# First dense products ahead of the second scores in the steps with few value groups; three value groups and the start of pair 7 moved into the first two steps

## The chip, the cores and the metric

The kernel runs on one core of a Trainium2 chip. Five engines work side by side, each through its own list of instructions in order: PE (matrix products; its weight loads are listed apart as PEld), DVE and ACT (elementwise work, reductions, copies out of PSUM), POOL (elementwise work in SBUF) and SP, which only issues DMAs. Time is device microseconds (us) of this core; the result of a kernel is the median of several runs. The profile is of one further execution.

## The reference, cut to what matters

```python
def _A_ref(x, mem0, Wq, Wk, Wv, Wo, seg_len):      # S=2048, Dm=512, H=32 heads of 128, M=8, seg 32
    mem = mem0
    for s in range(n_seg):                          # 64 segments
        h = concat([mem, x[:, 32*s:32*s+32]])       # 8 memory rows + 32 tokens
        q, k, v = h @ Wq, h @ Wk, h @ Wv
        p = softmax(mask(q k^T * scale))
        o = (p @ v) @ Wo
        mem = o[:, :8];  outs.append(o[:, 8:])
    return concat(outs)
def _B_ref(x, w1, w2):
    return relu(x @ w1) @ w2                        # 512 -> 1376 -> 512
x = x + _A_ref(layernorm(x), ...);  x = x + _B_ref(layernorm(x), ...)
x = x + _A_ref(layernorm(x), ...);  x = x + _B_ref(layernorm(x), ...)
```

The memory rows make the attention a recurrence over 64 segments, and there are two such layers with the same weights. Arithmetic is bf16 with f32 sums.

## The kernel before, in words

**Steps.** Step k (`step`, k = 1 to 67, after `first_step` for k = 0) does segment k of the first attention layer ("layer 0") and segment k-4 of the second ("layer 1") together, each 8 memory rows and 32 tokens. Steps 1 to 3 have layer 0 alone and steps 64 to 67 layer 1 alone (`single`). Beside the attention a step does the dense layer of the rows finished two steps before (`dense_h(k - 2)`, `dense_y(k - 2)`). What links one step to the next is `output_mem` (L564, tile wo: the memory rows' output product), a copy on ACT (L750, tile wm), a small turn on PE (L756, tile mt) and copies into HT and HTm, from which the next step's products start.

**Order inside a step.** PE, DVE, SP and POOL keep the order in which the program is written; only ACT's is chosen by a scheduler with priorities. For a step with both layers PE's order is: memory values (`memory_values`, L704), Q and K products of the first 16 heads (`qk`, L522, in batches of 6, 6 and 4 heads), filler (`block`), first scores (`scores`, L556: 16 products for layer 0, then 16 for layer 1), Q and K of the other 16 heads, filler, second scores, filler, the first part of `dense_y` (L482), `transpose_p(1)` (L598, tile tp), the rest of `dense_y`, `weighted_v` (L624, tile pv), `output_mem`, values of the second layer (L345), mt. Before each half's scores DVE writes the mask into the scores' PSUM bank (`masks`, L548), after the casts of K (L530); the second scores of layer 1 wait for their own mask. After the second scores DVE takes the maximum (L572), subtracts (L576), ACT takes the exponential (L578), DVE sums (L583), takes the reciprocal (L584) and multiplies (L588, into P1; POOL does it for layer 0). PE then turns P1, and ACT and DVE copy a half each into PT_sb (L602). In steps k = 5, 9, ..., 49 `moments_x` (L231, L218, L220) stands on DVE between the multiplication and its PT_sb copy.

**Filler.** `block` gives PE the output product of the token rows of the step before (L364 or L392) and, in steps k = 1, 5, 9, ..., 61, value groups (`values0`, L304). The values of the token rows in segments 2 and 3 of each four are computed for a pair of segments (pair 1, 3, ..., 31) at once: a group is one pair times 1024 columns of Wv, 8 products of 512 columns, one copy on ACT and two DMAs (L312) to a DRAM buffer, from which the steps load them into Vs. A pair has 4 groups, and there are 64 in all: 8 in `first_step`, 4 in step 1, 3 in each of steps 5 to 33, and 4 in each of steps 37 to 61 (`values_at`). A step with 3 groups, and step 1, is "light" (`split`): group 0 stands ahead of the scores, half before the first and half before the second, and the other groups after the second scores, behind `dense_h`. In the other steps with both layers `dense_h(k - 2)` stands ahead of the second scores. It makes 11 blocks of 128 dense columns (L464, tile hp): blocks 8 to 10 (12 products) first, then blocks 0 to 7 (32 products), each lot with its relu on ACT (L467, L469).

**The first steps and SP.** All loads and stores stand in SP's one list. In `first_step` it holds the loads of Wq, Wk, Wv in halves, Wo in four parts of 8 heads (L148), then the stores of what `first_step` makes: memory values (vmd, L709), values of segment 1 (vd_second, L350) and the groups (vd, L312). Behind these come, for step 1, the load of the rows of x for pair 7 (xb, L107), the load of step 1's values (Vs from vd_second, L678), two stores and two loads of the memory rows' values (vmd, L709; Vs from vmd, L714), the dense weights (L156 to L159), and the stores of step 1's groups. Each DMA takes the next of eight semaphores and is not issued before the DMA eight places ahead of it, which used the same one, has landed. In `first_step` `output_mem` is done in four parts of 8 heads, as Wo arrives, with one group ahead of each of the first two parts. What `first_step` makes is staged in the SBUF of the dense weights, which are loaded later.

**Pair 7** lies in the fourth block of 128 rows of x (n = 3 in `load_xb`, `moments_x`, `normalize`, `inputs_T`). Before the change this block is loaded in step 1, normalized at its end, turned by a DMA in step 3, and used from step 5 on.

Of the kernel before, what the change touches and what calls it, by code (L numbers as in the profile page):

```python
# [7 lines left out]
BF = mybir.dt.bfloat16  # L8
# [14 lines left out]
def kernel(  # L23
# [14 lines left out]
    nc = tc.nc  # L38
# [63 lines left out]
    xbs = {}  # L102

    def load_xb(n):
        tag, bufs = ("vst", 5) if n in (1, 2) else ("xb", 1)
        xbs[n] = wk.tile([128, Dm], BF, tag=tag, bufs=bufs, name="xb")
        nc.sync.dma_start(out=xbs[n][:], in_=A_x[0, 128 * n:128 * n + 128, :])  # L107

# [19 lines left out]
    Wv_v = A_Wv.rearrange("(c p) h e -> p c (h e)", p=128)  # L128
    Wo_v = A_Wo.rearrange("h e d -> e h d")
    PW = H * Dh // 2  # L130
    hh = H // 4

    def load_w(W_sb, W_v, pc):
        nc.sync.dma_start(out=W_sb[:, :, pc * PW:(pc + 1) * PW], in_=W_v[:, :, pc * PW:(pc + 1) * PW])  # L134
# [7 lines left out]
    def load_rest():  # L142
        load_xb(2)
        load_w(Wq_sb, Wq_v, 1)
        load_w(Wk_sb, Wk_v, 1)
        load_w(Wv_sb, Wv_v, 1)
        for pc in range(4):
            nc.sync.dma_start(out=Wo_sb[:, pc * hh:(pc + 1) * hh, :], in_=Wo_v[:, pc * hh:(pc + 1) * hh, :])  # L148

    w1_sb = const.tile([128, NC4, Dff], BF)  # L150
    w2_sb = const.tile([128, NFC, Dm], BF)
# [82 lines left out]
    def transpose_pe(xn):  # L234
        tp = ps_fill.tile([128, NC4, 128], BF, tag="fill", name="tpx")
        for c4 in range(NC4):
            nc.tensor.transpose(tp[:, c4, :], xn[:, c4 * 128:(c4 + 1) * 128], ident[:])
        return tp

    def inputs_T(n):  # L240
        xT0[n] = wk.tile([128, NC4, 128], BF, tag="xT0", bufs=3, name="xT0")
        if n < 3:
            tp = transpose_pe(xbs.pop(n))
            nc.scalar.copy(out=xT0[n][:], in_=tp[:])
        else:
            nc.sync.dma_start_transpose(out=xT0[n][:], in_=xbs.pop(n)[:])

# [46 lines left out]
    def values0(p, n, lo=0, hi=NC4, pool=None, stage=None):  # L294
        r = 64 * (p % 2)
        if (n, lo) == (0, 0):
            vd0[p] = dram.tile([64, H * Dh], BF, tag="vd0", bufs=3, name="vd0")
        if lo == 0:
            pool, tag = (pool, "wo") if pool else (ps_fill, "fill")
            vp_tiles[p, n] = pool.tile([128, 512], F32, tag=tag, name="vp")  # L300
        vp = vp_tiles[p, n]
        for c4 in range(lo, hi):
            for j in range(2):
                nc.tensor.matmul(vp[64 * j:64 * j + 64, :], lhsT=xT0[p // 2][:, c4, r:r + 64],  # L304
                                 rhs=Wv_sb[:, c4, (n + j) * 512:(n + j + 1) * 512],
                                 start=(c4 == 0), stop=(c4 == NC4 - 1), tile_position=(0, 64 * j))
        if hi < NC4:
            return
        vst = wk.tile([128, 512], BF, tag="vst", bufs=5, name="vst")[:] if stage is None else stage
        nc.scalar.copy(out=vst, in_=vp[:])  # L310
        for j in range(2):
            nc.sync.dma_start(out=vd0[p][:, (n + j) * 512:(n + j + 1) * 512], in_=vst[64 * j:64 * j + 64, :])  # L312
# [133 lines left out]

    def dense_h(d):
        if not 0 <= d <= LAST:  # L450
            return
        lo, hi = span(d)
        n = hi - lo

        def cols(c4):
            return xnT_tiles[d + 2][:, c4, lo:hi]

        hT = hT_tiles[d] = wk.tile([128, NFC, 64], BF, tag="hT", bufs=1, name="hT")
        for f0, f1 in ((8, NFC), (0, 8)):
            hp = ps_fill.tile([128, 8, 64], F32, tag="fill", name="hp")  # L460
            for fc in range(f0, f1):
                fs = 128 if fc < NFC - 1 else F_LAST
                for c4 in range(NC4):
                    nc.tensor.matmul(hp[0:fs, fc - f0, 0:n], lhsT=w1_sb[:, c4, fc * 128:fc * 128 + fs],  # L464
                                     rhs=cols(c4), start=(c4 == 0), stop=(c4 == NC4 - 1))
            nfull = min(f1, NFC - 1) - f0
            nc.scalar.activation(out=hT[:, f0:f0 + nfull, 0:n], in_=hp[:, 0:nfull, 0:n], func=ACTF.Relu)  # L467
            if f1 == NFC:
                nc.scalar.activation(out=hT[0:F_LAST, NFC - 1, 0:n], in_=hp[0:F_LAST, nfull, 0:n], func=ACTF.Relu)  # L469
# [90 lines left out]
    def output_mem(k, wo, h0=0, h1=H):  # L560
        n, c = divmod(k % 4, 2)
        for h in range(h0, h1):
            j = h % 4
            nc.tensor.matmul(wo[32 * j:32 * j + 32, :], lhsT=OTm[:, h, n, 2 * M * c:2 * M * c + 4 * M], rhs=Wo_sb[:, h, :],  # L564
                             start=(h < 4), stop=(h >= H - 4), tile_position=(0, 32 * j))
# [153 lines left out]
    def block(k, lo, hi):  # L719
        output_x(k - 1, lo, hi)  # L720
        groups = values_at(k)
        if split(k):

            rest = [(i, 0, NC4) for i in range(1, len(groups))]
            todo = [(0, 0, 2)] if lo == 0 else [(0, 2, NC4)] if hi == 16 else rest
        else:
            todo = [(i, c4, c4 + 2) for i in range(len(groups)) for c4 in range(0, NC4, 2)
                    if lo < 8 * i + 2 * c4 + 2 <= hi]
        for i, c_lo, c_hi in todo:
            p, n = groups[i]  # L730
            values0(p, n, c_lo, c_hi, ps_wo if i in (0, 2 if len(groups) == 3 else 3) else None)

    def split(k):
        return k == 1 or len(values_at(k)) == 3

    def values_at(k):


        if k == 1:
            return [(5, 4), (5, 6), (3, 4), (3, 6)]  # L740
        if k % 4 != 1 or not has0(k + 1):
            return []
        groups = [(p, n) for p in range(7, NSEG // 2, 2) for n in range(0, NCH, 2)]
        i = k // 4 - 1
        lo = 3 * min(i, 8) + 4 * max(i - 8, 0)
        return groups[lo:lo + (3 if i < 8 else 4)]

# [35 lines left out]
    def first_step():  # L783


        slots = iter([w1_flat[:, 512 * i:512 * i + 512] for i in range(NC4 * Dff // 512)] +
                     [w2_flat[:, 512 * i:512 * i + 512] for i in range(4)])
        masks(0)
        with tc.high_priority(offset=PRIO):
            qks = qk(0, [0])  # L790
            scores(qks, [0])
            softmax(0, [0], True)
            values_first(0)
            memory_values(0, (next(slots), None), (0,))
            values_second(0, next(slots))
            values0(1, 0, stage=next(slots))
            values0(1, 2, stage=next(slots))
            m = moments_x(2)
            normalize(nc.vector, xbs[2], xbs[2], m, 0, 128)
# [12 lines left out]
            nc.gpsimd.tensor_copy(out=HTm[:, :, 2 * M:32], in_=spare_T(1))  # L812
            values_second(1, next(slots))
            pvs = weighted_v([0])
            outputs(0, pvs)
            wo = ps_wo.tile([128, Dm], F32, tag="wo", name="wo")
            for i in range(4):
                if i < 2:
                    values0(1, 4 + 2 * i, stage=next(slots))
                output_mem(0, wo, 8 * i, 8 * i + 8)  # L820
            new_memory(0, [0], wo)
            output_ride(0)
            prepare(1)

    def step(k):
# [4 lines left out]
        has_x = n_x < NXT  # L830
        by_pe = k in (1, LAST)
        ahead = has1(k + 1) or not cont
        if has_x and (k % 4 == 0 or k == 1):
            load_xb(n_x)
        with tc.high_priority(offset=PRIO):
            qks = qk(0, act, behind=norm_rows.pop(k, None))
            load_values(k, act)
            if k == 1:
                memory_values(k)
        part = 8 if single else 5  # L840

        light = split(k)
# [16 lines left out]
        if single:  # L859
            block(k, part, 16)  # L860
        elif light:
            block(k, part, 16)
        else:
            dense_h(k - 2)
        with tc.high_priority(offset=PRIO):
# [2 lines left out]
        if single:  # L868
            if k < LAST:
                dense_h(k - 2)  # L870
            block(k, 16, H)
        elif light:
            dense_h(k - 2)
            block(k, 16, H)
        else:
            block(k, part, H)
# [14 lines left out]
        with tc.high_priority(offset=PRIO):  # L891
            pvs = weighted_v(act)
            outputs(k, pvs)
        if k == 1:
            normalize(nc.vector, xbs[n_x], xbs[n_x], moments_x(n_x), 0, 128)
        if single and k < LAST and ahead:
            add_dense(k - 2)
            store(k - 2)
# [106 lines left out]
```

## Time and profile before

| | us |
|---|---|
| median of 3 runs (1609.02 to 1609.59) | 1609.05 |
| the profiled execution | 1606.63 |
| its span, first to last instruction | 1604.8 |
| PE busy | 1568.6 |
| DVE busy | 1263.6 |
| ACT busy | 739.6 |
| POOL busy | 347.3 |
| step 1, from mt to mt (51.09 to 70.72) | 19.63 |
| step 5, with 3 groups (132.47 to 155.71) | 23.24 |
| step 33, with 3 groups (786.66 to 809.75) | 23.09 |
| step 37, with 4 groups (879.91 to 903.36) | 23.45 |

A step is measured here from the start of its own mt (L756), which opens it on PE, to the next one. In the timeline a row is the start, the time taken (from the first to the last of a run of like instructions), the engine, the line, the operation with its tiles and shape, and in brackets how long the engine had been idle before and for what. Rows named SPq show how long the queue's instruction took to issue, not when the data landed. The time of a PE row includes the way through the array, so that rows overlap: what a run of products costs is the distance to the next row's start.

### The profile page before, as it was taken

How to read it: one execution, taken by the hardware profiler on the slowest of the kernel's cores; microseconds unless marked ns; L12 is line 12 of the kernel's file. 1: busy time of each engine (PE TensorE's matmuls, PEld its weight loads, DVE VectorE, ACT ScalarE, POOL GpSimd, SP SyncE). 2: the span in 40 equal slices, each digit the busy share in tenths (PEclk: the TensorE clock that was granted, in tenths of full speed). 3: DMA queues.
4: the chain of work that ended last, by engine and by line, in shares of the span. 5: the costliest groups of instructions: out<-in, count | busy, mean ns of one | idle time of the engine just before them, and what ended most of it. 6: DMA issues, size and time to landing. Idle time of an engine off the chain costs nothing.

```text
span 1604.8 us, 94988 instructions
## 1 busy us (share of the span) xinstructions
PE 1568.6 (98%) x42778; PEld 1324.1 (83%) x42778; DVE 1263.6 (79%) x3113; ACT 739.6 (46%) x1799; POOL 347.3 (22%) x666
## 2 busy tenths in 40 slices
PE   6899999999999999999999999999999999999997
PEld 4577888888888888888888888888888888888876
DVE  4478888888888888888888888878888887787765
ACT  3335445444544544454444445444444544444442
POOL 2012222222222222222222222222222222222110
PEclk9999999999999999999999999999999999999999
DMA  9733343343344434433433443343343334334231
GB/s 368 218 87 74 78 86 89 65 97 85 82 72 89 87 65 96 86 79 75 91 88 64 98 86 80 77 90 90 64 100 82 81 74 87 90 57 99 72 72 32
DMA packets 216294, 146.41 MB, mean 91 GB/s; under 512 B 124968, under 2 KB 209232, under 8 KB 214864
## 3 DMA queue, kind: packets, MB, share of 16 engines
q1 hardware_dynamic: 212816, 136.13, 37.5%
q8 instruction: 336, 5.51, 1.5%
q0 software_dynamic: 3072, 4.20, 1.1%
q14 instruction: 70, 0.57, 0.1%
HBM read 65.41 MB, written 45.35 MB: 69 GB/s over the span
## 4 chain that ended last, share of the span: by engine, by line
PE 92%; DVE 3%; SPq 2%; DMA 1%; issue 1%; ACT 1%; POOLq 0%; POOL 0%; DVEq 0%; ACTq 0%
PE qp L522 35%; PE wox L364 10%; PE wo L564 8%; PE vm L704 7%; PE v L345 7%; PE hp L464 6%; PE sp L482 5%; PE pv L624 4%; PE sp L556 4%; PE vp L304 3%; PE tp L598 1%; SPq L148 1%; PE xp L438 1%; DMA Wo_sb<-in_A_Wo_dram 1%; SPq L134 1%
## 5 line engine op out<-in xcount | busy, mean ns | idle before, releaser
L528 ACT CAST QT<-qp 128x480 bf16<-128x480 f32 (+3 forms) x408 | 201.5, 494 | 394.6 <-PE qp L522 394.4
L522 PE MATMUL qp<-HT,Wq_sb 128*128 128x80 bf16 (+1 forms) x8704 | 370.7, 200 | 2.2 <-POOL HT L693 1.2
L522 PE MATMUL qp<-HT,Wk_sb 128*128 128x80 bf16 (+1 forms) x8704 | 369.6, 200 | 1.7 <-issue 1.2
L522 PEld LDWEIGHTS <-Wq_sb 128*128 128x128 bf16 x8704 | 326.7, 100 | 34.0 <-issue 26.7
L522 PEld LDWEIGHTS <-Wk_sb 128*128 128x128 bf16 x8704 | 328.9, 100 | 2.9 <-issue 2.5
L530 DVE CAST KT<-qp 128x480 bf16<-128x480 f32 (+3 forms) x408 | 225.3, 565 | 104.0 <-PE qp L522 101.6
L588 POOL TENSOR_TENSOR P_sb<-es,sm 128x320 bf16<-128x320 f32 x185 | 130.8, 721 | 751.2 <-ACT es L578 498.9
L364 PE MATMUL wox<-Wo_sb,OTx 128*64 128x256 bf16 x2880 | 173.7, 273 | 0.0
L572 DVE TENSOR_REDUCE mx<-sp 128x8 f32<-128x320 f32 x256 | 115.5, 487 | 73.6 <-PE sp L556 73.1
L364 PEld LDWEIGHTS <-OTx 128*64 128x64 bf16 x2880 | 150.2, 110 | 3.0
L583 DVE TENSOR_REDUCE sm<-es 128x8 f32<-128x320 f32 x256 | 118.6, 463 | 42.7 <-ACT es L578 32.8
L704 PE MATMUL vm<-Wv_sb,HTm 128*32 128x512 bf16 x2176 | 136.3, 380 | 0.8 <-DVE HT L770 0.8
L578 ACT ACTIVATE es<-es 128x320 f32<-128x320 f32 x256 | 110.2, 469 | 54.1 <-DVE es L576 52.9
L564 PE MATMUL wo<-Wo_sb,OTm 128*32 128x512 bf16 x2144 | 128.7, 381 | 3.4 <-DMA Wo_sb<-in_A_Wo_dram 3.4
L345 PE MATMUL v<-Wv_sb,xnT 128*32 128x512 bf16 x2048 | 128.9, 378 | 0.0
L548 DVE CAST sp<-maskb 128x320 f32<-128x320 bf16 x256 | 118.3, 483 | 0.0
L576 DVE TENSOR_TENSOR es<-sp,mx 128x320 f32<-128x320 f32 x256 | 113.6, 482 | 1.6
L704 PEld LDWEIGHTS <-HTm 128*32 128x32 bf16 x2176 | 89.8, 96 | 28.5 <-issue 11.6
L482 PE MATMUL sp<-w_sb,hT 128*64 128x256 bf16 (+4 forms) x1474 | 105.2, 276 | 1.2 <-ACT hT L467 1.2
L708 ACT CAST VmS<-vm 128x512 bf16<-128x512 f32 x134 | 78.6, 586 | 55.4 <-PE vm L704 54.2
L464 PE MATMUL hp<-xnT,w_sb 128*128 128x64 bf16 (+3 forms) x2948 | 100.7, 193 | 1.0 <-ACT xnT L964 0.7
L464 PEld LDWEIGHTS <-w_sb 128*128 128x128 bf16 (+1 forms) x2948 | 94.5, 101 | 1.9 <-issue 1.3
(109 smaller groups left out, 2027.9 us busy)
## 6 DMA issues: line engine op xcount, KB each, us to landing
Vs<-vd SPq DMA_DIRECT2D x96, 256.0 KB
vmd<-VmS SPq DMA_DIRECT2D x134, 128.0 KB
vd<-vst SPq DMA_DIRECT2D x128, 128.0 KB
Vs<-vmd SPq DMA_DIRECT2D x254, 32.0 KB
Vs<-vmd SPq DMA_DIRECT2D x60, 128.0 KB
vd<-vst SPq DMA_DIRECT2D x112, 64.0 KB
Wq_sb<-in_A_Wq_dram SPq DMA_DIRECT2D x2, 2048.0 KB
Wk_sb<-in_A_Wk_dram SPq DMA_DIRECT2D x2, 2048.0 KB
```

Of the source, the lines that this page charges most:

```text
L345: nc.tensor.matmul(vp[32 * j:32 * j + 32, :], lhsT=tokens[:, c4, :], rhs=Wv_sb[:, c4, n * 512:(n + 1) * 512], start=(c4 == 0), stop=(c4 == ...
L364: nc.tensor.matmul(out[64 * j:64 * j + nr, 0:256], lhsT=lhsT, rhs=rhs[:, 256 * j:256 * j + 256], start=start, stop=stop, tile_position=(0, ...
L464: nc.tensor.matmul(hp[0:fs, fc - f0, 0:n], lhsT=w1_sb[:, c4, fc * 128:fc * 128 + fs], rhs=cols(c4), start=(c4 == 0), stop=(c4 == NC4 - 1))
L482: nc.tensor.matmul(sp_banks[bank][64 * j:64 * j + n, 0:w], lhsT=hT_tiles[d][0:fs, fc, 0:n], rhs=w2_flat[0:fs, fc * Dm + 256 * j:fc * Dm + ...
L522: nc.tensor.matmul(qp[:, hi, 0:ncol], lhsT=W_sb[:, c4, h * Dh:(h + 1) * Dh], rhs=HT[:, c4, a_lo:a_hi, :], start=(c4 == 0), stop=(c4 == NC4 ...
L528: nc.scalar.copy(out=dst[:, 0:nh, a_lo * L:a_hi * L], in_=qp[:, 0:nh, 0:ncol])
L530: nc.vector.tensor_copy(out=dst[:, 0:nh, a_lo * L:a_hi * L], in_=qp[:, 0:nh, 0:ncol])
L548: nc.vector.tensor_copy(out=sp_tiles[a], in_=maskb2)
L564: nc.tensor.matmul(wo[32 * j:32 * j + 32, :], lhsT=OTm[:, h, n, 2 * M * c:2 * M * c + 4 * M], rhs=Wo_sb[:, h, :], start=(h < 4), stop=(h > ...
L583: nc.vector.tensor_reduce(out=sm[:], in_=es[:], axis=AX.X, op=ALU.add)
L588: eng.tensor_tensor(out=P, in0=es[:], in1=sm[:].unsqueeze(2).to_broadcast([128, 8, L]), op=ALU.mult)
L704: nc.tensor.matmul(vp[32 * j:32 * j + 32, :], lhsT=HTm[:, c4, :], rhs=Wv_sb[:, c4, n * 512:(n + 1) * 512], start=(c4 == 0), stop=(c4 == NC ...
```

## The change

Three things are done at once.

1. In light steps the first lot of dense products (blocks 8 to 10) is put between group 0's second half and the second scores; the other lot stays behind them. A step with 2 groups now counts as light too.
2. Three more groups are computed in `first_step`: (3, 4), (3, 6) and (5, 4), as pair and first column chunk. Wo arrives in five parts (8, 8, 8, 4 and 4 heads), and `output_mem` follows these, with one group ahead of each of the first three parts and two ahead of the fourth. All three are stores in SP's list ahead of step 1's loads.
3. Step 1 makes three groups instead of four: (5, 6), and the first two of pair 7, (7, 0) and (7, 2). For that x's rows of pair 7 are loaded behind Wo, normalized on DVE behind the first batch of step 1's Q and K, and turned on PE in step 1 (4 products and a copy on ACT) into a tile of their own; the turn by DMA in step 3 stays. The rows keep one of the five staging buffers (`vst`) until then. Step 1 has no group ahead of its first scores any more. Step 5 now makes 2 groups, steps 9 to 37 make 3, and steps 41 to 61 make 4: against before, steps 1, 5 and 37 make one group less.

```diff
     def load_xb(n):
-        tag, bufs = ("vst", 5) if n in (1, 2) else ("xb", 1)
+        tag, bufs = ("vst", 5) if n in (1, 2, 3) else ("xb", 1)
...
-    hh = H // 4
+    WO_PARTS = ((0, 8), (8, 16), (16, 24), (24, 28), (28, 32))
...
-        for pc in range(4):
-            nc.sync.dma_start(out=Wo_sb[:, pc * hh:(pc + 1) * hh, :], in_=Wo_v[:, pc * hh:(pc + 1) * hh, :])
+        for h0, h1 in WO_PARTS:
+            nc.sync.dma_start(out=Wo_sb[:, h0:h1, :], in_=Wo_v[:, h0:h1, :])
+        load_xb(3)
...
-    def inputs_T(n):
-        xT0[n] = wk.tile([128, NC4, 128], BF, tag="xT0", bufs=3, name="xT0")
-        if n < 3:
-            tp = transpose_pe(xbs.pop(n))
+    def inputs_T(n, early=False):
+        tag, bufs = ("ob", 1) if early else ("xT0", 3)
+        xT0[n] = wk.tile([128, NC4, 128], BF, tag=tag, bufs=bufs, name="xT0")
+        if n < 3 or early:
+            tp = transpose_pe(xbs[n])
...
-    def dense_h(d):
+    def dense_h(d, parts=(0, 1)):
...
-        for f0, f1 in ((8, NFC), (0, 8)):
+        for f0, f1 in [((8, NFC), (0, 8))[i] for i in parts]:
...
             rest = [(i, 0, NC4) for i in range(1, len(groups))]
-            todo = [(0, 0, 2)] if lo == 0 else [(0, 2, NC4)] if hi == 16 else rest
+            if k == 1:
+                todo = [] if lo == 0 else [(0, 0, 2)] if hi == 16 else [(0, 2, NC4)] + rest
+            else:
+                todo = [(0, 0, 2)] if lo == 0 else [(0, 2, NC4)] if hi == 16 else rest
...
     def split(k):
-        return k == 1 or len(values_at(k)) == 3
+        return len(values_at(k)) in (2, 3)
...
-        if k == 1:
-            return [(5, 4), (5, 6), (3, 4), (3, 6)]
+        if k in (1, 5):
+            return [(5, 6), (7, 0), (7, 2)] if k == 1 else [(7, 4), (7, 6)]
...
-        groups = [(p, n) for p in range(7, NSEG // 2, 2) for n in range(0, NCH, 2)]
-        i = k // 4 - 1
+        groups = [(p, n) for p in range(9, NSEG // 2, 2) for n in range(0, NCH, 2)]
+        i = k // 4 - 2
...
-            for i in range(4):
-                if i < 2:
-                    values0(1, 4 + 2 * i, stage=next(slots))
-                output_mem(0, wo, 8 * i, 8 * i + 8)
+            for groups, heads in zip((((1, 4),), ((1, 6),), ((3, 4),), ((3, 6), (5, 4)), ()), WO_PARTS):
+                for p, n in groups:
+                    values0(p, n, stage=next(slots))
+                output_mem(0, wo, *heads)
...
-        if has_x and (k % 4 == 0 or k == 1):
+        if k % 4 == 0 and has_x:
             load_xb(n_x)
         with tc.high_priority(offset=PRIO):
-            qks = qk(0, act, behind=norm_rows.pop(k, None))
+            behind = norm_rows.pop(k, None)
+            if k == 1:
+                def behind():
+                    normalize(nc.vector, xbs[n_x], xbs[n_x], moments_x(n_x), 0, 128)
+            qks = qk(0, act, behind=behind)
             load_values(k, act)
             if k == 1:
                 memory_values(k)
+                inputs_T(n_x, True)
...
         elif light:
             block(k, part, 16)
+            dense_h(k - 2, (0,))
...
         elif light:
-            dense_h(k - 2)
+            dense_h(k - 2, (1,))
             block(k, 16, H)
...
-        if k == 1:
-            normalize(nc.vector, xbs[n_x], xbs[n_x], moments_x(n_x), 0, 128)
```

More of the change, by code (lines that the diff above doesn't have):

```diff
@@ L238, in transpose_pe @@
         return tp
-    def inputs_T(n):
-        xT0[n] = wk.tile([128, NC4, 128], BF, tag="xT0", bufs=3, name="xT0")
-        if n < 3:
-            tp = transpose_pe(xbs.pop(n))
+    def inputs_T(n, early=False):
[3 more added lines that the diff above has]
+            tp = transpose_pe(xbs[n])
             nc.scalar.copy(out=xT0[n][:], in_=tp[:])
         else:
-            nc.sync.dma_start_transpose(out=xT0[n][:], in_=xbs.pop(n)[:])
+            nc.sync.dma_start_transpose(out=xT0[n][:], in_=xbs[n][:])
     def norm_parts(k):
@@ L456, in cols @@
             return xnT_tiles[d + 2][:, c4, lo:hi]
-        hT = hT_tiles[d] = wk.tile([128, NFC, 64], BF, tag="hT", bufs=1, name="hT")
-        for f0, f1 in ((8, NFC), (0, 8)):
+        if 0 in parts:
+            hT_tiles[d] = wk.tile([128, NFC, 64], BF, tag="hT", bufs=1, name="hT")
+        hT = hT_tiles[d]
+        for f0, f1 in [((8, NFC), (0, 8))[i] for i in parts]:
             hp = ps_fill.tile([128, 8, 64], F32, tag="fill", name="hp")
@@ L730, in block @@
             p, n = groups[i]
-            values0(p, n, c_lo, c_hi, ps_wo if i in (0, 2 if len(groups) == 3 else 3) else None)
+            values0(p, n, c_lo, c_hi, ps_wo if i in (0, 3 if len(groups) == 4 else 2) else None)
     def split(k):
-        return k == 1 or len(values_at(k)) == 3
+        return len(values_at(k)) in (2, 3)
     def values_at(k):
-        if k == 1:
-            return [(5, 4), (5, 6), (3, 4), (3, 6)]
+        if k in (1, 5):
+            return [(5, 6), (7, 0), (7, 2)] if k == 1 else [(7, 4), (7, 6)]
         if k % 4 != 1 or not has0(k + 1):
             return []
-        groups = [(p, n) for p in range(7, NSEG // 2, 2) for n in range(0, NCH, 2)]
-        i = k // 4 - 1
+        groups = [(p, n) for p in range(9, NSEG // 2, 2) for n in range(0, NCH, 2)]
+        i = k // 4 - 2
         lo = 3 * min(i, 8) + 4 * max(i - 8, 0)
@@ L786, in first_step @@
         slots = iter([w1_flat[:, 512 * i:512 * i + 512] for i in range(NC4 * Dff // 512)] +
-                     [w2_flat[:, 512 * i:512 * i + 512] for i in range(4)])
+                     [w2_flat[:, 512 * i:512 * i + 512] for i in range(8)])
         masks(0)
```

## The prediction

> **What bounds the kernel now.** The page's first part comes first:
>
> ```profile
> PE 1568.6 (98%) x42778; PEld 1324.1 (83%) x42778; DVE 1263.6 (79%) x3113; ACT 739.6 (46%) x1799; POOL 347.3 (22%) x666
> ```
>
> PE has next to no idle time over the whole, and its chain of waits gives PE 92%. So work taken off PE pays, unless something else is late in that very place. There are two such places: the first two steps, where data still arrives, and the second half of a light step. In `first_step` the timeline shows PE waiting for Wo:
>
> ```profile
> 46.86 0.61 PE L564 MATMUL wo<-Wo_sb,OTm 128*32 128x512 bf16 x8 [1.23 <-DMA Wo_sb<-in_A_Wo_dram]
> 49.59 0.82 PE L564 MATMUL wo<-Wo_sb,OTm 128*32 128x512 bf16 x8 [2.12 <-DMA Wo_sb<-in_A_Wo_dram]
> ```
>
> In all 3.35 us are free there. SP's own rows show what stands behind:
>
> ```profile
> 49.57 5.28 SPq L312 DMA_DIRECT2D vd<-w_sb  x7
> ...
> 56.07 2.71 SPq L312 DMA_DIRECT2D vd<-w_sb  x4
> 58.88 0.53 SPq L107 DMA_DIRECT2D xb<-in_A_x_dram  x1
> 59.58 0.34 SPq L678 DMA_DIRECT2D Vs<-vd_second  x1
> 60.01 0.87 SPq L709 DMA_DIRECT2D vmd<-VmS  x2
> 63.18 1.93 SPq L714 DMA_DIRECT2D Vs<-vmd  x2
> ```
>
> SP issues without a pause from 49.57 to 59.58, on stores whose data had long been staged. It is late, and step 1's loads of Vs queue behind. PE's rows show when they are needed:
>
> ```profile
> 66.96 0.57 PE L624 MATMUL pv<-PT,Vs 40*128 40x40 bf16 x16
> 67.59 0.56 PE L624 MATMUL pv<-PT_sb,Vs 40*128 40x40 bf16 x16
> 68.08 1.91 PE L564 MATMUL wo<-Wo_sb,OTm 128*32 128x512 bf16 x32
> ```
>
> The trace's landing records put the two Vs<-vmd loads at 65.01 and 66.68. The second has 67.59 - 66.68 = 0.9 us to spare, and no more.
>
> In step 33, a light one, PE's rows are:
>
> ```profile
> 800.52 0.42 PE L556 MATMUL sp<-KT,QT 128*40 128x40 bf16 x16
> 801.12 0.38 PE L556 MATMUL sp<-KT,QT 128*40 128x40 bf16 x16 [0.18 <-DVE sp L548]
> 801.43 1.52 PE L464 MATMUL hp<-xnT,w_sb 128*128 128x64 bf16 x44
> ```
>
> The 32 second scores take 801.43 - 800.52 = 0.91, as those of layer 1 wait for DVE's mask (800.58, 0.48 long). In step 37, where the dense products stand ahead, they take 895.08 - 894.66 = 0.42. So 0.49 is lost in each light step. DVE's rows of the same step show what comes after:
>
> ```profile
> 800.98 1.04 DVE L572 TENSOR_REDUCE mx<-sp 128x8 f32<-128x320 f32 x2
> ...
> 804.30 0.62 DVE L588 TENSOR_TENSOR P_sb<-es,sm 128x320 bf16<-128x320 f32 x1
> 804.85 0.68 DVE L231 BATCH_NORM_STATS2 stats<-xb 128x6 f32<-128x512 bf16 x1
> ...
> 806.16 0.49 DVE L602 CAST PT_sb<-tp 128x320 bf16<-128x320 f32 x1 [0.22 <-PE tp L598]
> ```
>
> PT_sb's last half is done at 806.65; the heads that read it start at 806.86.
>
> **Dense products ahead (light steps 9 to 33, seven of them).** Twelve products cost 12/44 of step 37's 1.44 (893.22 to 894.66), 0.39. The scores then start at 800.91 and those of layer 1 at 801.12, when their mask is ready: PE gains the whole 0.49. But the maximum starts later: it began 0.22 after layer 0's last score (800.76); that score now falls at 801.11, so the maximum at 801.33 instead of 800.98. From the maximum to the last heads of `weighted_v` step 37 takes 900.46 - 895.08 = 5.38, with DVE running from the multiplication (898.51) through the three `moments_x` instructions into the PT_sb copy (to 900.41) without a pause. The changed ACT order puts a 0.58 relu between the two exponentials; step 37 has a 0.57 copy there, so its row fits. 801.33 + 5.38 = 806.71 against 806.86: **gain 0.15**, bounds 0 (the chain of this step, 0.1 longer) and 0.49 (PE alone). Seven: 1.05 (0 to 3.4).
>
> **Steps 5 and 37.** In step 5 the maximum moves from 146.79 to 147.12 in the same way; 147.12 + 5.38 = 152.50 against 152.83. A group less (0.87: 28 value products take 3.03 in step 37, 895.08 to 898.11) only makes PE wait for the same chain. I take 0.3 (0 to 0.87). Step 37 becomes light: its maximum falls 1.93 after the start of its last Q batch but one row, as above (801.33 - 799.40), so at 892.65 + 1.93 = 894.58 instead of 895.08: 0.5 (0.35 to 0.87).
>
> Together the steady steps give **1.85** (0.35 to 5.1).
>
> **Step 0.** (3, 4) fits into the first wait for Wo (0.87 of 1.23), the other two (1.73) into the second (2.12); behind the last landing stand 4 heads instead of 8: 0.45 earlier. These three groups' own cost is hidden by Wo, and would be 2.6 without it. The fuller stretch should also spare the half-speed clock that follows the waits now:
>
> ```profile
> 48.00:52.00 4.00, 1.62 (x28) 0.41 (x28) 0.33 (x2) 0.77 (x2) 0.00 (x0) 0.73 0.56 167
> 52.00:56.00 4.00, 4.00 (x123) 4.00 (x124) 1.74 (x4) 0.80 (x3) 0.00 (x0) 0.50 0.38 88
> 56.00:60.00 4.00, 4.00 (x100) 2.44 (x98) 1.12 (x3) 1.46 (x4) 0.00 (x0) 0.91 0.48 134
> ```
>
> These are the stretches' busy times and, third from the end, the granted clock: half from 49.84 (0.27 x 4 / 0.5 back from 52) to 56.7. Q and K of the first heads take 4.38 there (51.91 to 56.29) against 3.5 for the second (59.06 to 62.83 without a wait of 0.26): 0.9. With step 0's 0.45 and the group less (0.87), minus the turn on PE (0.4 for 4 products at 28.18), PE would be **1.8** early in step 1.
>
> **But all of this ends in a wait for Vs.** SP has six more stores ahead of Vs<-vd_second, 0.64 each (0.62 in step 33, three in 1.87; 0.70 and 0.77 with the hitches of the rows above): 3.84. Wo takes five places and xb one, so the landing that is eight places back lets one store less go before Wo has landed: 0.64 more. The load of xb is no longer there: -0.63. Together 3.85 (3.1 to 4.7). The chain store, landing, load behind it moves along: Vs lands at 66.68 + 3.85 = 70.5, or 69.2 if the one straggler of the second store (last of 16 parts at 64.81, the one before at 63.44) does not come again. I take the middle, 69.9: **2.3 late** against 67.59 (0.9 to 3.7). Behind the waiting products stand wo, mt and all of step 2; nothing else of PE can pass.
>
> PE would wait from about 65.2 (66.96 - 1.8) to 69.9 with only pv's first half in between (its load lands at 65.01 + 3.85), which is longer than the 1.23 + 2.12 that brought half speed before. What it costs: a 512-column product takes 0.59 in the slow stretch (L438, 51.22) and 0.38 outside (70.84), 0.21 more; wo is 8 rounds of four such products side by side, 1.7, and the memory values another 1.7. The stretch lasted 6.9 us. I take **1.4** (0 to 3.4), most of wo's part, as wo starts soon after the wait.
> The Trainium skill ("TensorE: Matmul & The Clock Gate", Part 1: The HAM clock gate) says that the clock falls to half after at least one idle window of about 3.4 us, and that these windows run freely. By that a wait of 4.7 us need not hold a whole idle window, and the term could be 0. The trace disagrees as to "idle": the waits of 1.23 and 2.12 had 0.6 us of products between them, and half speed came all the same.
>
> Small: DVE's normalization of pair 7 (69.12 to 71.30) no longer stands ahead of step 1's copy into HTm, 0.15; in step 2 the dense products wait 0.30 for the turned rows, which come earlier by the two stores (of step 1's fourth group) that SP no longer has, 0.3. xb keeps one of five staging buffers until step 3: the copies that must wait for a buffer (second memory values of step 2, which waited for a store's landing at 76.9) wait as before relative to SP; 0, at worst 0.5.
>
> **Sum.** 2.3 + 1.4 - 0.15 - 0.3 - 1.85 = +1.4 on the profiled execution's 1606.6 (span 1604.8 and 1.8 around it), 1608.0; the runs' median lies 2.4 higher at 1609.05, so **1610.5**.
>
> **Rivals.** A measurement of this kernel can tell about 0.2% (3.2 us) from no change; the classes below go by that.
> - No half speed after the wait: 1610.5 - 1.4 = 1609.1. For it: the granted clock stays at 1.00 from 60 to 72 through waits of up to 0.7 (step 1's end), so not every wait brings it. The rule of the Trainium skill above would allow it too. Chance 0.15, no change.
> - The light steps gain all that PE loses (7 x 0.49 + 0.49 + 0.87 = 4.8), if the softmax chain is shorter than in step 37: 1607.5. Against it: that step's last heads start 0.05 after PT_sb, at the chain's limit. 0.12, no change.
> - Step 1 does not wait, if SP's late start is made good: -1.8 - 0.45 (small terms) - 1.85 = -4.1, 1605.0. Against it: the unbroken SP rows. 0.13, faster.
> - **Slower:** SP's backlog in step 1 at its full length (3.7) and half speed through wo and the memory values (3.4): 1609.05 + 7.1 - 0.45 - 1.85 = 1613.9. It decides once wait and slow clock together pass 5.5 us. 0.18, slower.
> - The change does not do what it says, as the groups fail to fit the waits for Wo and push mt back: wait for Vs unchanged, about 1610. 0.02.
> - The forecast, 1610.5: 0.40.
>
> Faster 0.13, within 0.2% 0.69, slower 0.18. The range runs from 1605.5 to 1613.9, leaving out the third rival's (0.13) and the upper part of the fourth's (0.07).
>
> **What would show it.** Step 1: pv's second half idle for DMA Vs<-vmd or vmd until about 70, SP's Vs<-vd_second row near 63.4, granted clock near half behind it, step 1 longer than 19.63 by some 4 us. Step 0: no wait for Wo over 0.5, no half speed at 50. Light steps: scores 32 in a row, no wait for the mask, step length 23.09 falling to about 22.95, the last heads right behind PT_sb; step 37 near 22.95. It is wrong if Vs lands before PE gets there, or if light steps fall below 22.8.

## The result and the profile after

The changed kernel takes 1611.7 us (median of 10 runs, 1609.99 to 1616.07); beside it the kernel before took 1608.21 (10 runs, 1605.12 to 1609.59). The ratio is **1.0029, 95% interval 1.0021 to 1.0038**: slower by 0.29%. The profiled execution took 1610.73, with a span of 1608.9 against 1604.8: 4.1 us more.

The page's first part hardly moves. PE is busy 2.3 us longer (1568.6 before), which says nothing of where:

```profile
PE 1570.9 (98%) x42782; PEld 1323.0 (82%) x42782; DVE 1262.5 (78%) x3113; ACT 737.5 (46%) x1800; POOL 346.7 (22%) x666
```

So the steps were measured one by one, from mt to mt. Lengths in us, each of one execution (e1 to e11 are the runs of the next section):

| | before | after | e1 | e2 | e3 | e4 | e7 | e9 | e11 |
|---|---|---|---|---|---|---|---|---|---|
| step 1 begins at | 51.09 | 50.44 | 51.66 | 50.62 | 51.15 | 50.53 | 50.76 | 50.75 | 50.79 |
| step 1 | 19.63 | 25.23 | 19.33 | 25.98 | 20.64 | 23.07 | 25.71 | 18.42 | 18.42 |
| step 2 | 19.25 | 18.55 | 23.95 | 19.16 | 26.35 | 20.66 | 20.48 | 19.22 | 19.92 |
| step 4 begins at | 109.02 | 113.05 | 113.99 | 114.92 | 116.96 | 113.71 | 115.77 | 107.20 | 107.95 |
| step 5 | 23.25 | 23.68 | 23.08 | 22.65 | 23.08 | 23.46 | 22.90 | 23.75 | 23.58 |
| a light step (17, 33) | 23.09 | 23.17 | 23.17 | 23.09 | 23.17 | 23.18 | 22.96 | 23.17 | 22.96 |
| step 37 | 23.45 | 23.18 | 23.45 | 23.09 | 23.17 | 23.17 | 22.96 | 23.17 | 22.96 |

Two columns explain the 4.1. Step 4 begins 4.0 later, and step 1 alone is 5.6 longer (steps 0, 2 and 3 give back 1.6). A light step is 0.09 longer instead of shorter.

**The first steps.** PE's timeline of the changed kernel:

```profile
46.74 0.61 PE L568 MATMUL wo<-Wo_sb,OTm 128*32 128x512 bf16 x8
47.29 1.92 PE L306 MATMUL vp<-Wv_sb,xT 128*64 128x512 bf16 x16
49.14 0.62 PE L568 MATMUL wo<-Wo_sb,OTm 128*32 128x512 bf16 x8
50.44 0.27 PE L763 MATMUL mt<-sel,wm 128*32 128x16 bf16 x16 [0.69 <-ACT wm L757]
...
64.86 0.48 PE L602 MATMUL tp<-ident,P_sb 128*64 128x80 bf16 x16 [0.60 <-DVE P_sb L592]
70.36 0.69 PE L628 MATMUL pv<-PT,Vs 40*128 40x40 bf16 x16 [5.02 <-DMA Vs<-vmd]
70.89 0.70 PE L628 MATMUL pv<-PT_sb,Vs 40*128 40x40 bf16 x16
71.52 3.42 PE L568 MATMUL wo<-Wo_sb,OTm 128*32 128x512 bf16 x32
75.67 0.27 PE L763 MATMUL mt<-sel,wm 128*32 128x16 bf16 x16 [0.74 <-ACT wm L757]
```

The waits for Wo are gone: the groups fill them, and step 1 opens 0.65 earlier. PE reaches the heads of `weighted_v` at 65.34 (70.36 less 5.02), 1.6 earlier than before, and then sits for 5.02 us. The product wo takes 3.42 instead of 1.91. SP's rows show what held the values back:

```profile
44.56 10.32 SPq L314 DMA_DIRECT2D vd<-w_sb  x12
54.97 0.54 SPq L713 DMA_DIRECT2D vmd<-w_sb  x1
55.60 1.61 SPq L352 DMA_DIRECT2D vd_second<-w_sb  x1
57.30 7.22 SPq L314 DMA_DIRECT2D vd<-w_sb  x10
64.62 0.52 SPq L682 DMA_DIRECT2D Vs<-vd_second  x1
65.23 0.90 SPq L713 DMA_DIRECT2D vmd<-VmS  x2
68.21 0.67 SPq L718 DMA_DIRECT2D Vs<-vmd  x2
```

Twenty-two group stores (16 before) occupy SP from 44.56 to 64.52. Among the first five of them it waits three times for a landing of Wo, 2.2 us in all (once, 1.0, before); from 49.32 on it issues without a pause. The load of Vs from vd_second, issued at 59.58 before, goes at 64.62, and the two loads from vmd, issued at 63.18 and 64.83 before, go at 68.21 and 68.59. The windows (span, PE, PEld, DVE, ACT and POOL busy, granted clock, DMA share, GB/s) show the clock:

```profile
48.00:52.00 4.00, 2.99 (x67) 1.56 (x64) 1.00 (x3) 1.91 (x4) 0.00 (x0) 1.00 0.55 161
64.00:68.00 4.00, 0.74 (x20) 0.36 (x16) 1.23 (x4) 0.45 (x2) 0.00 (x0) 0.97 0.65 174
68.00:72.00 4.00, 1.64 (x40) 1.35 (x44) 0.64 (x3) 1.21 (x3) 0.00 (x0) 0.50 0.51 136
72.00:76.00 4.00, 3.26 (x49) 1.08 (x41) 0.65 (x2) 0.58 (x1) 0.00 (x0) 0.67 1.04 394
```

Half speed has moved: none at 50 any more, but from 67.8 to 74.6, over heads and wo.

**A light step.** PE and then DVE in step 33 (take 5.23 off to stand beside the rows of before):

```profile
805.30 0.62 PE L306 MATMUL vp<-Wv_sb,xT 128*64 128x512 bf16 x4
805.85 0.59 PE L468 MATMUL hp<-xnT,w_sb 128*128 128x64 bf16 x12
806.37 0.57 PE L560 MATMUL sp<-KT,QT 128*40 128x40 bf16 x32
806.88 1.11 PE L468 MATMUL hp<-xnT,w_sb 128*128 128x64 bf16 x32
...
812.16 0.37 PE L628 MATMUL pv<-PT_sb,Vs 40*128 40x40 bf16 x16
```

```profile
806.79 0.89 DVE L576 TENSOR_REDUCE mx<-sp 128x8 f32<-128x320 f32 x2 [0.49 <-PE sp L560]
...
810.62 0.69 DVE L232 BATCH_NORM_STATS2 stats<-xb 128x6 f32<-128x512 bf16 x1
811.63 0.48 DVE L606 CAST PT_sb<-tp 128x320 bf16<-128x320 f32 x1
```

The scores stand 32 in a row, with no wait for the mask: they take 0.51 instead of 0.91. But the maximum starts at 806.79, which is 801.56 on before's scale, where it started at 800.98. From it to the last heads it is 5.37 us, with PT_sb done at 812.11 and the heads at 812.16. The step ends by the softmax chain, and that chain starts 0.58 later.

### The profile page after: what moved, and what is told of

Same layout as the page of the kernel before. It is cut to its first block, busy times and chain, and to the rows that moved or that the text cites. A ratio compares the mean times of both kernels' runs of the same rounds, so it can differ in the third digit from the quotient of the medians.

```text
span 1608.9 us, 94994 instructions
## 1 busy us (share of the span) xinstructions
PE 1570.9 (98%) x42782; PEld 1323.0 (82%) x42782; DVE 1262.5 (78%) x3113; ACT 737.5 (46%) x1800; POOL 346.7 (22%) x666
## 4 chain that ended last, share of the span: by engine, by line
PE 95%; DMA 2%; DVE 1%; SPq 1%; ACT 1%; issue 1%; POOLq 0%; DVEq 0%; ACTq 0%
PE qp L526 38%; PE wox L366 10%; PE wo L568 8%; PE vm L708 7%; PE v L347 7%; PE hp L468 6%; PE sp L486 5%; PE pv L628 4%; PE sp L560 4%; PE vp L306 3%; DMA Wv_sb<-in_A_Wv_dram 2%; PE tp L602 1%; PE xp L440 1%; SPq L134 0%; PE mt L763 0%
```

## The experiments

All ratios are against the kernel before, run beside each.

**e1_dense_only: the dense order alone.** Before, with only the dense products split (`load_xb`, groups and Wo as before).

```diff
         elif light:
             block(k, part, 16)
+            dense_h(k - 2, (0,))
...
-            dense_h(k - 2)
+            dense_h(k - 2, (1,))
```

> The kernel before with the first part of the change alone: in the light steps 5 to 33 the first 12 dense products stand ahead of the second scores. My theory now (from step 33 of both traces): PE loses some 0.1 us at each change between the value groups' half-width products and full-width ones, so the scores start later than by the 12 products alone, and the softmax chain behind them (5.38 us from the maximum to the last heads) decides: each of the eight light steps 23.17 instead of 23.09 us, +0.7 us in all, about 1608.9. Rival one, the prediction on record: each light step 0.15 faster, -1.2 us in all. Rival two, the changed place costs only together with the other parts (fewer groups, other stores): light steps as before, 23.09.

Measured: 1609.63 against 1608.41, ratio 1.0005 (0.9994 to 1.0016); light steps 23.17, just as after. So this part alone makes a light step 0.09 longer, whatever stands in step 1. The profile had a surprise elsewhere: step 2, whose code is before's, took 23.95, waiting for the turned rows:

```profile
86.44 1.39 PE L466 MATMUL hp<-xnT,w_sb 128*128 128x32 bf16 x44 [3.14 <-DMA xnT<-XN]
```

SP's lateness in the first steps thus differs from execution to execution of the same code, and one profile of them is one draw.

**e2_early_only: the rest alone.** After, with `dense_h(k - 2)` whole behind the second scores again.

> The changed kernel without the dense products ahead of the scores (parts two and three of the change alone). My theory: the wait for Vs in step 1 and the half-speed clock behind it are all here: step 1 again about 25.2 us from mt to mt, step 4 begins about 4.0 us later than in the kernel before, light steps 9 to 33 back at 23.09, step 5 with two groups some 0.5 shorter than 23.25 and step 37 23.09 instead of 23.45: in all +3 us, about 1611. Rival: most of the loss comes from the dense products' new place and what it does to ACT's order; then this runs within 1 us of the kernel before.

Measured: 1611.48, ratio 1.0021 (1.0010 to 1.0033); step 1 25.98, light steps 23.09. Most of the loss (0.21 of 0.29%) is in the early part; in this execution step 4 begins 5.9 later than in before's.

**e3_defer: the added stores later.** After, with the stores of the three added groups kept back: four of the six behind step 1's two stores of the memory rows' values, two behind its loads.

```diff
             transpose_step(k)
+            if k == 1:
+                late.pop(0)()
+                late.pop(0)()
             load_memory_values(k, act)
+            if k == 1:
+                late.pop(0)()
```

> The changed kernel, with nothing else moved than the six added stores in SP's list: four go behind step 1's two stores of the memory rows' values, where SP waits for their landing anyway, and two behind the loads that follow. My theory: the place of the stores makes the wait. Vs<-vd_second is issued near 60 instead of 64.6, the second Vs<-vmd lands near 66.5, PE waits 1 to 2 us there instead of 5.0, the granted clock stays at 1.00, wo takes 1.9 instead of 3.4: step 1 about 19.5, step 4 begins 0 to 1 us earlier than in the kernel before (the dense weights are issued 1.4 us later, which may give back up to 2 us in step 2). In all 3 to 5 us faster than the changed kernel, about 1607.5. Rival: the wait comes from the early start of pair 7 (its load behind Wo, the buffer that it keeps, its normalization ahead of the casts of K); then PE still waits until about 70 and the time stays near 1611.7.

Measured: 1611.96, ratio 1.0024 (1.0013 to 1.0036). A miss, and the most useful one. PE's timeline shows the wait of step 1 cut to 2.19, wo at 1.91 again, and a new wait one step on:

```profile
68.25 0.56 PE L636 MATMUL pv<-PT,Vs 40*128 40x40 bf16 x16 [2.19 <-DMA Vs<-vmd]
...
69.15 1.91 PE L576 MATMUL wo<-Wo_sb,OTm 128*32 128x512 bf16 x32
...
88.71 1.55 PE L476 MATMUL hp<-xnT,w_sb 128*128 128x32 bf16 x44 [3.69 <-DMA xnT<-XN]
```

Step 1 is 4.6 shorter than after's, step 2 7.8 longer: half speed, too, now stands behind the new wait (87.64 to 94.47). SP has the same number of DMAs to issue, so its lateness shows at a later load. But this execution took 1614.81, 2.9 above the run's median, and not all of the new wait is SP's order: PE comes 1.8 earlier than in after (85.02 against 86.81), the load of the turned rows is through SP at 84.58, only 0.2 later, and it lands 4.1 us behind that (88.66) instead of 1.5 (85.91). Had it landed as fast, the wait would be about 1.1; why it did not is not shown.

**e4_busy: no half speed.** After, with 20 products of 512 columns ahead of step 1's `weighted_v`, whose output nobody reads.

> The changed kernel with 20 products of 512 columns (128x128 weights) put on PE ahead of step 1's weighted_v, written to a PSUM tile that nobody reads: work that is not part of the computation, some 4.3 us in the 5.0 us of the wait. My theory: the half-speed clock behind the wait comes from PE's idleness; kept busy, wo takes 1.9 instead of 3.4 us, step 1 about 23.7 instead of 25.2, and the time falls by 1.5 us to about 1610.2 although there is more to do. Rival: the slow stretch does not hang on the wait, or 1.5 us of it is made good later; then wo stays at 3.4, or the total at 1611.7.

Measured: 1613.77, ratio 1.0034 (1.0023 to 1.0046).

```profile
65.59 4.26 PE L907 MATMUL idle<-Wv_sb,ident 128*128 128x512 bf16 x19 [0.16 <-issue]
70.04 0.55 PE L628 MATMUL pv<-PT,Vs 40*128 40x40 bf16 x16 [0.19 <-DMA Vs<-vmd]
...
70.95 1.91 PE L568 MATMUL wo<-Wo_sb,OTm 128*32 128x512 bf16 x32
...
80.86 0.62 PE L389 MATMUL wox<-Wo_sb,OTx 128*32 128x256 bf16 x15 [0.85 <-issue]
85.14 0.53 PE L526 MATMUL qp<-HT,Wq_sb 128*128 128x40 bf16 x15 [0.77 <-issue]
```

Keeping PE at work does remove the slow clock: no half-speed stretch there, heads and wo at full speed, step 1 shorter by 2.17. So idleness brings it, and in step 1 it costs about 1.8 (1.5 in wo, 0.25 in the heads; another 0.3 of the gain is loads that landed earlier). Yet the total did not gain: step 2 is 2.11 longer, 1.62 of it two stops amid like products that nothing in the profile releases. Whether these stops come from the edit stays open. They are not the whole answer: without them PE would have come to step 2's dense products at 85.23, and the turned rows land at 85.99 (85.91 in after, where PE comes at 86.81), so that SP would have kept all but some 0.8 of the gain.

**e5_one_store and e6_before_one_store: half the DMAs.** Each group's two stores as one DMA of shape 2 x 64 x 512, in after (e5) and in before (e6).

```diff
-        for j in range(2):
-            nc.sync.dma_start(out=vd0[p][:, (n + j) * 512:(n + j + 1) * 512], in_=vst[64 * j:64 * j + 64, :])
+        nc.sync.dma_start(out=vd0[p][:, n * 512:(n + 2) * 512].rearrange("t (j e) -> j t e", j=2), in_=vst)
```

> The changed kernel, with each value group stored by one DMA of 128 rows instead of two of 64 (the same bytes): 11 fewer DMAs in SP's list of the first step and 3 fewer in step 1. The runs so far say that moving the six stores only moves the wait (from step 1's Vs to step 2's turned rows), and that keeping PE busy in it gives nothing back. Theory now: what bounds steps 1 and 2 is the number of DMAs that SP has to issue, 0.64 us for each store of 64 rows, whatever PE does. A store of 128 rows takes 0.4 to 0.5 in the rows of vmd, so some 9 us of SP's time go: Vs<-vd_second is issued before 57 instead of 64.6, no wait for Vs in step 1 and none for xnT in step 2, no half speed, step 4 begins at 106 to 107 instead of 113.0: 6 us faster than the changed kernel, about 1605.5. Rival: the bytes or the landing of the stores bound it, not their number; then the wait for Vs stays within 1.5 us of what it was and the time near 1611.

> The kernel before, with each value group stored by one DMA of 128 rows instead of two of 64. Theory: SP was late in steps 1 and 2 here already (the wait for xnT in step 2, 0.3 us in one execution and 3.1 in another); with 12 DMAs fewer up to step 1's end that is gone, step 4 begins near 108 us in every execution: 1 to 3 us faster than before, about 1606. And with SP's lateness gone from both kernels, the changed one (the run beside this) should be the faster of the two, by the 1.5 to 2 us that the three groups save in steps 0 and 1. Rival: SP's lateness in the kernel before is an accident of single executions; then the time stays within 1 us of 1608.4.

Measured: 1644.47, ratio 1.0217 (1.0202 to 1.0232), and 1641.09, 1.0196 (1.0181 to 1.0212). Both far off. SP's rows of e5:

```profile
44.81 12.32 SPq L313 DMA_DIRECT2D vd<-w_sb  x6
...
61.40 10.72 SPq L313 DMA_DIRECT2D vd<-w_sb  x5
72.30 2.37 SPq L681 DMA_DIRECT2D Vs<-vd_second  x1
```

Half as many DMAs take longer than all of them did: 2.05 and 2.14 each, against 0.86 and 0.72 for one 64-row store in after. The landing records differ as well: such a store has three, the last two of them close together 7 to 11 us after its issue, and a 64-row one has 16, the last a median of 2.5 us after it. That fits 128 KB which, with a leading dimension of 2, moved in two pieces. This is no test of the number of issues; e9 is.

**e7_dense_first: the twelve products one place earlier.** After, with the first dense lot ahead of group 0's second half instead of behind it.

```diff
         elif light:
-            block(k, part, 16)
             dense_h(k - 2, (0,))
+            block(k, part, 16)
```

> The changed kernel with the first 12 dense products ahead of group 0's second half instead of behind it, in the light steps. Theory: each change on PE between full-width products (Q and K, dense) and half-width ones (groups, scores) costs some 0.1 us; the changed kernel has two such changes between group and scores that the kernel before had not. Here there is only one (dense to group), so the scores start 0.1 earlier, and steps 9 to 37 fall from 23.17 to about 23.07. Rival: the 0.1 comes from the dense products' own start (their weights or PSUM), wherever they stand: 23.17 stays.

One time, 1614.22, too little for the total; what it was made for is the steps: light steps 22.96, shorter by 0.215 than after's and by 0.13 than before's. The start of each single product in the trace shows the cause. Where PE goes from 128-column tiles (128*128 or 128*96) to half-width ones (128*64, 128*40), or back, the next product starts 0.09 to 0.10 later than among its like: in after's step 33 0.131 instead of 0.036 into the group, 0.311 instead of 0.213 out of it, 0.139 instead of 0.045 into the scores, 0.111 instead of 0.022 out of them. Group to scores, in before, costs nothing extra (0.213). So after crosses four times, before and e7 twice: two crossings, 0.19 of the 0.215.

**before_again.** The kernel before once more, one execution.

> The kernel before once more, for a second profile of its first steps. If SP's lateness there varies from one execution to the next, as the run with the dense products alone suggests (its first steps are the same as this kernel's, and step 4 began 5 us later there), then step 4 begins anywhere between 109 and 114 us here, with all of the difference in waits for DMAs in steps 1 to 4; the light steps stay at 23.08 to 23.09. If that run was an outlier, step 4 begins at 109.0 within 0.5.

1610.66; step 2 20.73 and step 4 at 110.73, against 109.02 in the first execution: the early part alone differs by 1.7 us between the two.

**e9_rows_after and e10_rows_before: the same bytes in half the DMAs, 128 rows each.** The DRAM buffer is laid out so that a group's store is one plain DMA of 128 rows; the load that reads it back takes as long as it did (medians in after and e9: 0.33 us to issue, 3.9 to land). e9 is after, e10 before with it.

```diff
-            vd0[p] = dram.tile([64, H * Dh], BF, tag="vd0", bufs=3, name="vd0")
+            vd0[p] = dram.tile([4, 2, 64, 512], BF, tag="vd0", bufs=3, name="vd0")
...
+        nc.sync.dma_start(out=vd0[p][n // 2].rearrange("j t e -> (j t) e"), in_=vst)
```

> The changed kernel, with a group's DRAM buffer laid out so that its store is one plain DMA of 128 rows (as those of vd_second and vmd are) and no shape of two by 64, which landed in 2 parts instead of 16 and took 2.6 us each in the two runs before. The loads of Vs read the same bytes in rows of 1 KB, as the other loads of Vs do. Theory, as before: SP's number of issues bounds steps 1 and 2. 11 issues fewer by the end of the first step, at 0.64 for two against 0.45 for one, put Vs<-vd_second before 58 instead of 64.6; no wait for Vs in step 1 beyond 0.5 us, none for xnT in step 2, no half speed; step 1 about 18.6, step 4 begins at 106 to 108 instead of 113.0, the time falls by 5 to 6 us to about 1606. Rival: landing of the bytes bounds it; then the wait stays near 4 to 5 us and the time near 1611.5.

> The kernel before with the same layout of the groups' buffers and one store of 128 rows for each. Theory: its steps 1 to 4 were late for SP too, by an amount that varies (step 4 began at 109.0, 110.7 and 114.0 in three executions of the same first steps); here step 4 begins near 108 and the time falls by 1 to 4 us to about 1606.5. The changed kernel with this layout should be level with it or up to 2 us faster. Rival: SP is not what bounds the first steps of the kernel before; then it stays at 1608 to 1609.

Measured: e9 1606.18 against 1607.53, ratio 0.9987 (0.9977 to 0.9998); e10 1606.45, 0.9989 (0.9978 to 1.0001). SP and then PE in e9:

```profile
51.55 3.86 SPq L313 DMA_DIRECT2D vd<-w_sb  x5
55.59 0.33 SPq L681 DMA_DIRECT2D Vs<-vd_second  x1
56.67 1.64 SPq L714 DMA_DIRECT2D vmd<-VmS  x2
59.78 0.67 SPq L719 DMA_DIRECT2D Vs<-vmd  x2
```

```profile
65.17 0.48 PE L601 MATMUL tp<-ident,P_sb 128*64 128x80 bf16 x16 [0.60 <-DVE P_sb L591]
65.58 0.57 PE L627 MATMUL pv<-PT,Vs 40*128 40x40 bf16 x16
66.02 0.57 PE L627 MATMUL pv<-PT_sb,Vs 40*128 40x40 bf16 x16
66.52 1.91 PE L567 MATMUL wo<-Wo_sb,OTm 128*32 128x512 bf16 x32
69.16 0.27 PE L764 MATMUL mt<-sel,wm 128*32 128x16 bf16 x16 [0.73 <-ACT wm L758]
```

SP is through with the stores at 55.4 instead of 64.5, nothing waits for Vs, half speed does not occur there, step 1 is 18.42 and step 4 begins at 107.20. The bytes are the same: it is the number of issues that the change could not afford. For before a gain is not shown: the interval holds 1, step 4 begins at 109.75 in e10, between the 109.02 and 110.73 of before's two executions, and the waits for Wo and half speed at 50 stay. Between e9 and e10 the totals do not decide.

**e11_rows_dense_first: both repairs.** After with e9's layout and e7's order.

> The changed kernel with both mends: the groups' stores as one DMA of 128 rows, and the first dense products ahead of group 0's second half. The dense products' place alone took light steps from 23.17 to 22.96 (23.09 before the change), step 5 from 23.68 to 22.90. Theory: the two gains lie in different places and add: step 4 begins at 106 to 108, nine light steps 0.2 shorter than in the changed kernel: about 1604, faster than both kernels by 4 us or more. Rival: SP bounds the first steps by landings, or the light steps' stores delay a later load; then it stays above 1607.

Measured: **1602.93 (1601.85 to 1604.60) against 1607.53, ratio 0.9973 (0.9963 to 0.9984)**: it beats before, and by the ratios (1.0029) after too. PE in its step 33:

```profile
799.70 0.58 PE L467 MATMUL hp<-xnT,w_sb 128*128 128x64 bf16 x12
800.21 0.62 PE L306 MATMUL vp<-Wv_sb,xT 128*64 128x512 bf16 x4
800.67 0.56 PE L559 MATMUL sp<-KT,QT 128*40 128x40 bf16 x32
801.16 1.11 PE L467 MATMUL hp<-xnT,w_sb 128*128 128x64 bf16 x32
...
806.45 0.37 PE L627 MATMUL pv<-PT_sb,Vs 40*128 40x40 bf16 x16
```

From the first dense product to the first score it is 0.97 here and, with the same 16 products in the other order (805.30 to 806.37), 1.07 in after; the other 0.1 is the crossing into the group, which after pays ahead of its row. Against e9 it gains 3.2; the order accounts for 8 x 0.215 = 1.7 of that, and the rest lies within the two intervals.

## Why the prediction held, and where not

The forecast, 1610.5 and no change most likely, fell 1.2 short of 1611.7; the time is inside the range, and the loss is just on the other side of the 0.2% that parts "within" from "slower" (0.29%). The sum against the profiled execution was +1.4; it came to +4.1, and to +3.5 between the medians. That the time itself came closer is in part luck: the forecast put the median 2.4 above the profiled execution, and after's lay 1.0 above.

- **The wait for Vs: right in mechanism, short in size.** The chain was the one described, six more stores ahead of Vs<-vd_second. The load was put at 63.4 and went at 64.62: two of the 22 stores (1.18 and 1.54, against some 0.6) and the store to vd_second (1.61, against 0.41) took longer, where before has two such stores (1.58 and 0.93) in the same stretch. The heads' second half is late by 70.89 - 67.59 = 3.3, forecast 2.3 (0.9 to 3.7).
- **Half speed: right in place and size, but not a cost that adds up whole.** 1.4 was forecast for wo; it took 1.5 more (3.42 against 1.91). e4 removed it, and its step 1 gained 2.17, but no time was gained in the total; by the landing of the turned rows at most some 0.8 could have been gained in that execution. The rival without half speed is refuted by the windows. The half-speed stretches of the executions, but for the one in which each ends, last 3.41, 6.83, 10.24 (e6), 13.65 (e7) or 23.89 us (e5). The Trainium skill ("TensorE: Matmul & The Clock Gate", Part 1: The HAM clock gate) has the clock decided by windows of about 3.4 us, and these lengths are one, two, three, four and seven of 3.41: on that the traces agree.
- **Step 0 and the small terms: right in number.** 0.65 earlier (0.45 forecast), PE 1.6 early at the heads (1.8), no wait for Wo. Step 2's wait for the turned rows is gone (18.55), as forecast, but not because the rows come earlier: they land at 85.91, 3.2 later than before (82.72), and PE comes 4.4 later. In e1 and e3, where PE comes earlier, the wait is there (3.14 and 3.69).
- **The dense products ahead: this step failed.** "Twelve products cost 12/44 of step 37's 1.44, 0.39", and from it a gain of 0.15 a step. The chain behind the maximum was right to 0.01 (5.37 against 5.38). But the maximum was put at 801.33 and came at 801.56: the rate was taken from the middle of a run of like products, and the place between two half-width runs adds two crossings, 0.19. So each of the seven steps lost 0.09 instead of gaining 0.15. e7 and e11, without the two added crossings, gain 0.13, close to the forecast's 0.15.
- **Steps 5 and 37.** Step 37 gained 0.28, not 0.5, by the same 0.22. Step 5 was put at a gain of 0.3 and lost 0.44, but 0.61 of its 23.68 are two stops within Q and K products, one of which the timeline shows (the first of these rows; the second is the usual length of 24 such products):

```profile
146.07 1.32 PE L526 MATMUL qp<-HT,Wk_sb 128*128 128x80 bf16 x24
147.22 1.03 PE L526 MATMUL qp<-HT,Wq_sb 128*128 128x80 bf16 x24
...
155.93 0.48 PE L602 MATMUL tp<-ident,P_sb 128*64 128x80 bf16 x16 [0.83 <-DVE P_sb L592]
```

  These two stops are more than one draw: e9 and e11 have them at the same place, 10.2 to 10.3 and 13.3 to 13.4 us into the step, and 0.7 long together; e4 has one at 13.1, and the other executions have none in this step. Without them it is 23.07, a gain of 0.18, where e1, with three groups, has 23.08: with the dense products ahead the chain sets this step, and the group less buys nothing, as forecast. e2, with two groups and the dense products behind, has 22.65: there the order costs 0.42.
- **The sum.** Early part +4.0 (forecast 3.25); steady steps 7 x 0.09 - 0.18 - 0.28 = +0.2 (forecast -1.85); together 4.2, where the spans differ by 4.1. That these meet so closely is chance: steps 4 to 63 are 1.2 longer in all, 1.0 more than these terms, mostly stops in single steps, and steps 64 to 67, whose program is the same, are 1.1 shorter. Of the terms, most of the miss is the sign of the light steps.
- **The slower rival** named the right place and asked for wait and slow clock above 5.5 together; they came to 3.3 + 1.5 = 4.8, and it was the light steps that did not pay them back.

Still open: what stops PE for 0.1 to 1 us within runs of like products. Between steps 4 and 63 these stops in the Q and K products sum to 1.4 to 4.1 us an execution, in before as in after; some recur at the same place in executions of like programs, as in step 5, and most do not. The traces hold a lead that no run tests: of the 66 such stops in which the starts of two products lie over 0.25 us apart, in all executions but e5's and e6's, 43 end 0.9 to 1.9 us after a 16 KB transfer of the DMA queue named "q8 instruction" is over, where 22% of all Q and K products start in that distance. Instructions that arrive late are thus a candidate, and no more.

## What to carry to other kernels

Work moved into an engine's idle time still has to pay on the queue that carries its results: count the DMAs that are issued ahead of the next load that someone waits for, since in e3 moving them only moved the wait, and in e9 halving their number at the same bytes removed it. Price a moved run of products with the change of tile width at both its ends, and put it beside runs of its own width. Then look for what the step ends on: a gain on PE that delays the head of the softmax chain is a loss.

## What the runs showed of the hardware

- A store of shape 2 x 64 x 512 took SP 2.05 to 2.14 us on average in a row (e5), and its last two landing records came 7 to 11 us after the issue; the same bytes as one 128-row DMA took 0.77 (e9: 3.86 for 5, 1.91 of it one of them, the others about 0.4 each), and a 64-row store of half the bytes 0.72 to 0.86 (after).
- Each change between full-width and half-width tiles on PE cost 0.09 to 0.10 us between the starts of products (step 33 of after); from one half-width shape to the other (128*64 to 128*40) nothing beyond the 0.213 that a product of the group takes (step 33 of before).
- Products that nobody reads kept the granted clock at 1.00 through a wait of 5 us (e4), and the kernel was no faster for it.
